# Bounds of the later batches' x taken five steps behind their loads instead of three, with two steps more per batch

## The chip, the cores and the metric

The kernel runs on one core of one Trainium2 chip. The metric is the device time of one execution in microseconds (us). Three timed runs of the kernel before gave 1472.26, 1482.52 and 1481.33 us, median 1481.33. The profile shown below is of a separate execution that took 1473.78 us, 1472.0 us of it between its first and its last instruction.

The names of the engines: PE is the matrix engine (PEld its weight loads), DVE, ACT and POOL are the vector, scalar and GpSimd engines, SP is the engine whose queue issues every DMA of this kernel (SPq).

## The reference

```python
def reference(...):                      # x: (8, 3136, 256) float32
    F = (filt_r + 1j * filt_i)[None]     # filter over 1569 frequencies
    x = np.fft.irfft(np.fft.rfft(x, axis=1) * F, n=3136, axis=1)
    X = np.fft.fft(np.fft.fft(x, axis=1), axis=2)
    u = x + np.real(X)
    un = (u - mean(u)) / sqrt(var(u) + 1e-6)          # over the 256 channels
    return u + np.maximum(un @ w_ch1, 0) @ w_ch2      # 256 -> 1024 -> 256
```

## The kernel before

There are eight batches. Each goes forward (`there`) and home (`back`), and its tokens then go through the two products of the feed-forward part in 49 groups of 256 tokens. The FFT over 3136 tokens is split into stages that are small matrix products, with the transposes between stages done by storing to DRAM and loading back.

**Forward, per batch b** (`forward1`, then `forward2`). Seven tiles of x of 512 KB are loaded (line 398, names `x_b_0` to `x_b_6`). A bound of each tile is taken: for batches 1 and 2 on ACT by a sum of squares (line 404, `xsq`), for batches 3 to 7 on DVE by a reduction to the largest magnitude (line 413 calls `absmax`, whose instruction is line 282, written to `mx`). The bounds give the power of two `sx` by which x is scaled. Then there are 14 steps: x is scaled and split in two halves of 16 bits (lines 436 and 437, `x16`), multiplied (line 442, or line 428 for batches 1 and 2, `s1`), split again (lines 444 and 445, `ast`), and stored to the DRAM tensor `d1` (line 446 or 432). All 14 stores must have landed before the first of seven loads `at` (line 467) can read `d1` back; each of them feeds two `spectrum` steps (lines 492 and 493, product `s2`; lines 502 and 506 take it out of PSUM on DVE into `yt` and `t2`). The inverse transform follows (lines 562 to 564, `i1`, stored to `d2` as `bt`), then on the way home the loads `b2` from `d2` (line 605), the products `y` (line 628), ACT's scaling `ys` (line 637), and the stores to `dy` (line 611).

**The feed-forward part.** Group g has eight columns f. Per column there are six products `h` of 512 columns (line 839), a rectifier on ACT (line 848) and a remainder on DVE (line 849, which with line 848 releases one of two PSUM buffers of `h`), and twelve products `acc` of 256 columns (line 868). The loop over q = 8g + f (392 turns, two more to drain) writes one column of first products, one column of second products, and a few steps of the batches ahead. The group's input comes over a chain: `y` is fetched from `dy` (line 698), the channel transform `mix` (line 711) is added on DVE (line 721), normalised (`st`, `mv`, `sb`, `un`, `u16`), and transposed by a DMA (line 815, `ut`).

**What sets the order.** `forward1` and `forward2` are generators. Between two `yield`s lies one step, and `advance` runs them to a count that grows with q, from line 1050 on in the main loop. A batch has `STEPS` steps, and the loop writes `STEPS`/49 of them per turn once it is past its start (`STEPS`/28 in the first 39 turns). What is written so is given to a scheduler that simulates a timeline; it decides the final order of each engine's instructions. Each engine executes its list in that order, so an instruction that waits holds up all behind it on its engine.

```python
XLAG = 3
FIRST = 21 + XLAG
STEPS = FIRST + PAUSE + 7 * 5                 # 63
for q in range(7 + XLAG):                     # forward1
    if q < 7: nc.sync.dma_start(raw[q], a["x"][b, q])
    k = q - XLAG
    if k >= 0: ... bound of tile k ...
    if q < 6 + XLAG: yield
```

Batch 0 has its own first stage without a lag, and idles `PAUSE + XLAG - 1` steps so that its count comes out as `STEPS` too. The loads of the feed-forward weights (`raw`, line 911) hang on step numbers of batch 0. The x tiles, the `at` tiles, the `z` tiles and half of the `raw` tiles share seven buffers.

Of the kernel before, what the change touches and what calls it, by code (L numbers as in the profile page):

```python
# [33 lines left out]


PAUSE = 4
XLAG = 3
FIRST = 21 + XLAG
STEPS = FIRST + PAUSE + 7 * 5
WAIT = 2  # L40
# [158 lines left out]
def _program(ctx, tc, nc, a, NB):  # L199
# [24 lines left out]
    def after(*keys):  # L224

        order = ExitStack()
        for k in keys:
            if k in marks:
                order.enter_context(tc.issue_after(marks[k]))
        return order  # L230
# [50 lines left out]
    def absmax(dst, src, axis=AX.X):  # L281
        nc.vector.tensor_reduce(dst, src, axis=axis, op=ALU.max, apply_absolute_value=True)
# [107 lines left out]
    def forward1(b, d1):  # L390
        raw = [xp.tile([128, 4, 256], F32, tag="big", name=f"x_{b}_{q}") for q in range(7)]
        xs = [t[:112] for t in raw]
        m = tp.tile([112, 8], F32, tag="mx", name=f"mx_{b}")
        for q in range(7 + XLAG):
            with after(("y", 1), ("un", 0)) if b == 1 and q > 2 else after(("b", 1)) if b == 1 else nullcontext():
                if q < 7:
                    with after("sp") if b > 1 else nullcontext():
                        nc.sync.dma_start(raw[q], a["x"][b, q])
                k = q - XLAG
                if k >= 0 and b in SQUARED:  # L400
# [4 lines left out]
                elif k >= 0:  # L405
                    with after("h"):
                        absmax(m[:, k : k + 1], xs[k], AX.XY)
            if q < 6 + XLAG:
                yield
# [45 lines left out]
    def forward2(b, d1, d2):  # L455
# [118 lines left out]
        for c in range(far):  # L574
            load(c)
            if b:
                yield
        for _ in range(PAUSE - far if b else PAUSE + XLAG - 1):
            yield
# [545 lines left out]
```

## Time and profile before

| | value |
|---|---|
| timed runs | 1472.26, 1482.52, 1481.33 us |
| profiled execution | 1473.78 us, span 1472.0 us |
| mean granted TensorE clock | 0.993 |
| busy PE, PEld, DVE | 1420.6, 937.4, 1066.2 us |
| busy ACT, POOL | 766.9, 533.2 us |
| DMA | 280.55 MB, 191 GB/s on the mean |

PE is busy for 97% of the span by the page. The span has three parts: some 137 us in which batch 0 and the weights are prepared, the long middle in which the batches' transforms are mixed into the feed-forward part, and from about 1300 us an end in which there is feed-forward work alone. A row that says "waited for: total, times, longest" names the engine and line that waited, and what ended the wait last.

### The profile page before, as it was taken

To read this page: it belongs to the slowest core of one execution; us is meant where nothing else is said; L and a number is where in the kernel's file an instruction comes from. 1 tells how busy PE (TensorE), PEld (TensorE's weight loads), DVE (VectorE), ACT (ScalarE), POOL (GpSimd) and SP (SyncE) were. 2 spreads that over 40 slices of the span, in tenths; PEclk is the share of its full clock that TensorE was granted. 3 is DMA by queue.
4 is the path that set the end of the run, shared out by engine and by line. 5 is a ranking of instruction groups with operands and counts; after the bars stand their busy time and mean duration, and the time that the engine had idled before them with its cause. 6 is when DMAs were issued, how large, how long until landed. Compare 5 with 4: busy or idle time off the path is not lost.

```text
span 1472.0 us, 30599 instructions
## 1 busy us (share of the span) xinstructions
PE 1420.6 (97%) x11521; PEld 937.4 (64%) x11521; DVE 1066.2 (72%) x2341; ACT 766.9 (52%) x1420; POOL 533.2 (36%) x674
## 2 busy tenths in 40 slices
PE   7988999999999999999999999999999999999998
PEld 3734566556766676567756667666766667666666
DVE  6786687387878876987768876887769786545552
ACT  4757455546456554555537564565446554344341
POOL 3840096028510771038400673028500574010110
PEclk9999999999999999999999999999999999999999
DMA  8966687879976988589775997679684997553320
GB/s 332 325 176 199 181 171 192 237 201 240 205 226 170 217 194 232 159 214 234 163 239 157 233 203 213 182 200 249 153 248 139 212 220 160 140 140 96 87 58 29
DMA packets 445331, 280.55 MB, mean 191 GB/s; under 512 B 218944, under 2 KB 410752, under 8 KB 445184
## 3 DMA queue, kind: packets, MB, share of 16 engines
q1 hardware_dynamic: 445184, 278.61, 72.4%
q8 instruction: 90, 1.47, 0.4%
q14 instruction: 57, 0.47, 0.1%
HBM read 124.88 MB, written 102.79 MB: 155 GB/s over the span
## 4 chain that ended last, share of the span: by engine, by line
PE 64%; DMA 11%; DVE 9%; issue 6%; ACT 4%; POOL 3%; SPq 3%; DVEq 0%; ACTq 0%; POOLq 0%
PE h L839 24%; PE acc L868 24%; DMA x<-x 4%; PE s L442 3%; PE y L628 3%; DMA at<-d 2%; PE mix L711 2%; DVE y L721 2%; DMA d<-ast 2%; PE s L492 1%; PE i L562 1%; DVE h L849 1%; PE i L564 1%; PE i L563 1%; PE s L428 1%
## 5 line engine op out<-in xcount | busy, mean ns | idle before, releaser
L868 PE MATMUL acc<-w2s,h 128*128 128x256 f16 x4704 | 594.6, 273 | 4.8 <-ACT h L848 3.6
L839 PE MATMUL h<-ut,w1s 128*128 128x512 f16 x2352 | 580.8, 379 | 9.8 <-DVE h L849 6.9
L868 PEld LDWEIGHTS <-h 128*128 128x128 f16 x4704 | 455.4, 98 | 149.1 <-issue 14.9
L848 ACT ACTIVATE h<-h 128x512 f16<-128x512 f32 x392 | 232.8, 594 | 376.1 <-PE h L839 368.8
L849 DVE SCALAR_TENSOR_TENSOR h<-h,h 128x512 f16<-128x512 f32 x392 | 267.5, 684 | 203.4 <-ACT h L848 201.8
L839 PEld LDWEIGHTS <-w1s 128*128 128x128 f16 x2352 | 221.0, 98 | 217.9 <-issue 27.4
L808 POOL TENSOR_TENSOR u<-un,u 128x512 f16<-128x512 f32 x94 | 108.4, 1169 | 676.5 <-ACT u L806 659.9
L721 DVE SCALAR_TENSOR_TENSOR y<-mix,alpha,y 128x508 f32<-128x508 f32 (+1 forms) x368 | 156.0, 475 | 4.1 <-PE mix L711 2.6
L510 POOL TENSOR_TENSOR yt<-yt,t 128x224 f32<-128x224 f32 x112 | 76.4, 682 | 136.1 <-DVE t L506 88.4
L803 ACT ACTIVATE un<-y,sb 128x256 f32<-128x256 f32 x196 | 101.9, 590 | 37.7 <-DVE sb L796 32.4
L516 POOL TENSOR_TENSOR y<-yt,y 128x448 f16<-128x448 f32 x105 | 108.1, 1032 | 20.9 <-ACT y L515 18.7
L637 ACT ACTIVATE ys<-y,alpha 128x512 f32<-128x512 f32 x112 | 75.9, 684 | 70.6 <-PE y L628 69.2
L570 DVE TENSOR_TENSOR bt<-i,bt 112x512 f16<-112x512 f32 x112 | 75.7, 683 | 50.1 <-ACT bt L569 49.8
L502 DVE SCALAR_TENSOR_TENSOR yt<-s,pF,ft 128x448 f32<-128x448 f32 x112 | 75.4, 674 | 25.1 <-PE s L493 19.0
L569 ACT CAST bt<-i 112x512 f16<-112x512 f32 x112 | 64.4, 583 | 53.2 <-PE i L564 47.9
L877 DVE SCALAR_TENSOR_TENSOR y<-acc,beta,y 128x512 f32<-128x512 f32 x98 | 71.1, 744 | 26.1 <-PE acc L868 26.0
L515 ACT CAST y<-yt 128x448 f16<-128x448 f32 x112 | 62.7, 563 | 36.0 <-POOL yt L511 33.5
L628 PE MATMUL y<-b,i 112*64 112x512 f16 (+1 forms) x480 | 70.4, 377 | 8.5 <-DMA b<-d 7.3
L555 POOL TENSOR_TENSOR eo<-ef,eo 128x448 f16<-128x448 f32 (+6 forms) x62 | 60.8, 984 | 44.5 <-ACT eo L554 43.1
L506 DVE SCALAR_TENSOR_TENSOR t<-s,pF,ft 128x448 f32<-128x448 f32 x112 | 75.4, 674 | 0.0
L534 POOL TENSOR_TENSOR ef<-yt 128x224 f32<-128x224 f32 x112 | 74.2, 681 | 1.8
L511 POOL TENSOR_TENSOR yt<-yt,t 128x224 f32<-128x224 f32 x112 | 73.7, 660 | 0.5 <-DVE mv L781 0.5
(131 smaller groups left out, 1663.2 us busy)
## 6 DMA issues: line engine op xcount, KB each, us to landing
x<-x SPq DMA_DIRECT2D x56, 512.0 KB
at<-d SPq DMA_DIRECT2D x56, 512.0 KB
b<-d SPq DMA_DIRECT2D x56, 512.0 KB
d<-ast SPq DMA_DIRECT2D x112, 224.0 KB
d<-bt SPq DMA_DIRECT2D x112, 224.0 KB
out<-y SPq DMA_DIRECT2D x98, 256.0 KB
y<-dy SPq DMA_DIRECT2D x92, 256.0 KB
dy<-ys SPq DMA_DIRECT2D x208, 112.0 KB
```

Source lines behind the costliest of these rows:

```text
L510: nc.gpsimd.tensor_tensor(yh[:, 0], yh[:, 0], t2v[:, 1], op=ALU.subtract)
L516: last = half(b, hf == 1).tensor_tensor(ylo, ytv, yhi, op=ALU.subtract)
L570: marks["low"] = nc.vector.tensor_tensor(bt[:, :, 1], p, bt[:, :, 0], op=ALU.subtract).ins
L628: marks["i2"] = nc.tensor.matmul(p[64 * h : 64 * h + 64, js], i2[:, t, h, i], bt[:, o + js.start : o + js.stop, h], start=i == 0, stop=i == 1,
L637: nc.scalar.activation(ys[:, o : o + 2], p, AF.Copy, scale=al[:, 2:3])
L721: nc.vector.scalar_tensor_tensor(out, p, al, y, op0=ALU.mult, op1=ALU.add)
L803: nc.scalar.activation(un[:m, k], y[:m, t, k], AF.Identity, bias=sb[:m, i, 1:2], scale=sb[:m, i, 3:4])
L808: marks["u16", g] = low.tensor_tensor(u16[:m, :, :, 1], unv, u16[:m, :, :, 0], op=ALU.subtract).ins
L839: marks["pe"] = nc.tensor.matmul(p[:, c0 : c0 + n].rearrange("p (t k q) -> p t k q", k=2, q=m), w1s[:, d, hw, 128 * f : 128 * f + 128], ut ...
L848: nc.scalar.activation(h[:, 0, :nt], p[:, :nt], AF.Relu)
L849: marks["h"] = nc.vector.scalar_tensor_tensor(h[:, 1, :nt], p[:, :nt], 0.0, h[:, 0, :nt], op0=ALU.max, op1=ALU.subtract).ins
L868: nc.tensor.matmul(acc[:m, k], h[:, hh, c0 : c0 + m], w2s[:, f, hw], start=f == 0 and k == 0 and i == 0, stop=f == 7 and k == 1 and i == 2,)
```

## The change

It raises the lag between the load of an x tile and its bound from three steps to five, for batches 1 to 7; `FIRST` and `STEPS` follow (63 becomes 65), and batch 0 idles for two steps more.

```diff
 PAUSE = 4
-XLAG = 3
+XLAG = 5
 FIRST = 21 + XLAG
 STEPS = FIRST + PAUSE + 7 * 5
```

No instruction is added or removed: on each engine the same instructions stand in another order. Three places follow. Line and operation come first in a row, then what is written, what is read, and the shape; the last number of a name is a buffer's.

The first is DVE at the bounds of batch 4, amid the columns of group 15. Before:

```order
L849 SCALAR_TENSOR_TENSOR h16_15_0_7853<-h_15_0_7846,h16_15_0_7853 128x512
L282 TENSOR_REDUCE mx_4_7810<-x_4_0_7803 112x1
L849 SCALAR_TENSOR_TENSOR h16_15_1_7897<-h_15_1_7890,h16_15_1_7897 128x512
L877 SCALAR_TENSOR_TENSOR y_14_6561<-acc_14_0_7608,beta_95,y_14_6561 128x512
L877 SCALAR_TENSOR_TENSOR y_14_6561<-acc_14_1_7609,beta_95,y_14_6561 128x512
L282 TENSOR_REDUCE mx_4_7810<-x_4_1_7804 112x1
L849 SCALAR_TENSOR_TENSOR h16_15_2_7937<-h_15_2_7930,h16_15_2_7937 128x512
L282 TENSOR_REDUCE mx_4_7810<-x_4_2_7805 112x1
L849 SCALAR_TENSOR_TENSOR h16_15_3_7972<-h_15_3_7965,h16_15_3_7972 128x512
L282 TENSOR_REDUCE mx_4_7810<-x_4_3_7806 112x1
L849 SCALAR_TENSOR_TENSOR h16_15_4_8014<-h_15_4_8007,h16_15_4_8014 128x512
```

And of the change:

```order
L849 SCALAR_TENSOR_TENSOR h16_15_0_7853<-h_15_0_7846,h16_15_0_7853 128x512
L849 SCALAR_TENSOR_TENSOR h16_15_1_7896<-h_15_1_7889,h16_15_1_7896 128x512
L877 SCALAR_TENSOR_TENSOR y_14_6561<-acc_14_0_7608,beta_95,y_14_6561 128x512
L877 SCALAR_TENSOR_TENSOR y_14_6561<-acc_14_1_7609,beta_95,y_14_6561 128x512
L849 SCALAR_TENSOR_TENSOR h16_15_2_7935<-h_15_2_7928,h16_15_2_7935 128x512
L282 TENSOR_REDUCE mx_4_7810<-x_4_0_7803 112x1
L282 TENSOR_REDUCE mx_4_7810<-x_4_1_7804 112x1
L849 SCALAR_TENSOR_TENSOR h16_15_3_7972<-h_15_3_7965,h16_15_3_7972 128x512
L282 TENSOR_REDUCE mx_4_7810<-x_4_2_7805 112x1
L849 SCALAR_TENSOR_TENSOR h16_15_4_8012<-h_15_4_8005,h16_15_4_8012 128x512
```

The first bound moved behind two more columns, the second behind one, the third behind one; the last of the seven (not shown) stands behind one column more. Batches 6 and 7 look alike; in batch 3 the first bound moves by two columns and the last by none; in batch 5 none moves by more than one and the first and last not at all. The loads of x stand in the same places of SP's list, but for the seventh, which goes ahead of one load of `b2`, in batches 3 to 7.

The second is ACT at the bounds of batch 2 (`xsq_2_0` to `xsq_2_6`), amid the columns of group 4, with the first scalings of batch 1 on its way home (`ys_1_0`). Before:

```order
L848 ACTIVATE h16_4_2_3537<-h_4_2_3530 128x512
L404 ACTIVATE xsq_2_0_3315,mx_2_3275<-x_2_0_3268 112x1024
L637 ACTIVATE ys_1_0_3352<-y_1_0_3353,alpha_1_2161 128x512
L637 ACTIVATE ys_1_0_3352<-y_1_1_3363,alpha_1_2161 128x512
L404 ACTIVATE xsq_2_1_3345,mx_2_3275<-x_2_1_3269 112x1024
L404 ACTIVATE xsq_2_2_3348,mx_2_3275<-x_2_2_3270 112x1024
L848 ACTIVATE h16_4_3_3601<-h_4_3_3594 128x512
```

And of the change:

```order
L848 ACTIVATE h16_4_2_3525<-h_4_2_3518 128x512
L848 ACTIVATE h16_4_3_3595<-h_4_3_3588 128x512
L848 ACTIVATE h16_4_4_3637<-h_4_4_3630 128x512
L404 ACTIVATE xsq_2_0_3344,mx_2_3275<-x_2_0_3268 112x1024
L404 ACTIVATE xsq_2_1_3414,mx_2_3275<-x_2_1_3269 112x1024
L637 ACTIVATE ys_1_0_3348<-y_1_0_3349,alpha_1_2161 128x512
L637 ACTIVATE ys_1_0_3348<-y_1_1_3359,alpha_1_2161 128x512
L404 ACTIVATE xsq_2_2_3416,mx_2_3275<-x_2_2_3270 112x1024
```

Both the bounds and the first scalings of batch 1 moved back by two columns; the seventh bound moved from behind column 6 of group 4 to behind column 0 of group 5. On PE the first product `y_1_0` moved from behind the third `h` column of group 4 into its sixth.

The third is DVE where the first spectrum of batch 5 (`yt_5_0`) is taken out, amid the last columns of group 23 (in both kernels the last remainder of the stage before, `ast_5_13`, stands just ahead of `h16_23_4`). Before:

```order
L849 SCALAR_TENSOR_TENSOR h16_23_6_11241<-h_23_6_11234,h16_23_6_11241 128x512
L780 BN_STATS st_25_11157<-y_25_10903 128x6 x2
L781 BN_AGGR mv_25_11156<-st_25_11157 128x2 x2
L792 RECIPROCAL sb_25_11166<-sb_25_11166 128x4
L793 SCALAR_TENSOR_TENSOR sb_25_11166<-sb_25_11166 128x4
L849 SCALAR_TENSOR_TENSOR h16_23_7_11300<-h_23_7_11293,h16_23_7_11300 128x512
L794 SCALAR_TENSOR_TENSOR sb_25_11166<-mv_25_11156,sb_25_11166 128x4
L795 SCALAR_TENSOR_TENSOR sb_25_11166<-sb_25_11166 128x4
L796 SCALAR_TENSOR_TENSOR sb_25_11166<-mv_25_11156,sb_25_11166 128x4
L502 SCALAR_TENSOR_TENSOR yt_5_0_11180<-s2_5_0_0_11181,pF_115,ft_91 128x448
```

And of the change:

```order
L849 SCALAR_TENSOR_TENSOR h16_23_6_11215<-h_23_6_11208,h16_23_6_11215 128x512
L780 BN_STATS st_25_11157<-y_25_10881 128x6 x2
L781 BN_AGGR mv_25_11156<-st_25_11157 128x2 x2
L792 RECIPROCAL sb_25_11166<-sb_25_11166 128x4
L793 SCALAR_TENSOR_TENSOR sb_25_11166<-sb_25_11166 128x4
L502 SCALAR_TENSOR_TENSOR yt_5_0_11180<-s2_5_0_0_11181,pF_115,ft_91 128x448
```

The spectrum now stands ahead of the remainder of column 7. On PE the products between the last `s1` of a batch and its first `s2` change with it. In batch 4 they were 18 `h`, 46 `acc` and 4 `y` (and 16 small ones of `mix`), and are 15, 35 and 4; in batch 5 they were 23, 52 and 8, and are 19, 36 and 4; in batch 6 they were 17, 36 and 8, and are 18, 46 and 4; in batch 7 they were 21, 52 and 8, and are 18, 37 and 4.

## Rows read from the trace of the kernel before

**Rows 1.** Busy time by stretch: start and end (us), length, then for PE, PEld, DVE, ACT and POOL the busy us with the count of instructions, then the granted clock, the DMA share and GB/s. The first row is the middle, the second the end without transforms, the third lies in the first stage of batch 7.

```profile
137.00:1300.00 1163.00, 1137.58 (x9454) 762.37 (x9454) 878.84 (x1926) 622.04 (x1156) 456.46 (x578) 1.00 0.79 198
1300.00:1460.00 160.00, 160.00 (x1162) 107.99 (x1161) 82.65 (x199) 58.48 (x108) 13.62 (x12) 1.00 0.30 79
1120.00:1140.00 20.00, 20.00 (x127) 12.12 (x126) 19.77 (x46) 12.77 (x22) 0.00 (x0) 1.00 0.46 133
```

**Rows 2.** Waits of PE between 137 and 1472 us, all that are listed: who waited for whom, then us in total, times, and the longest.

```profile
PE s L492 <- DMA at<-d: 7.0, 9, 1.9
PE h L839 <- DVE h L849: 4.9, 5, 1.7
PE i L562 <- DMA z<-y: 4.5, 6, 1.4
PE y L628 <- DMA b<-d: 3.1, 4, 1.5
PE h L839 <- DMA ut<-u: 2.3, 2, 1.5
PE acc L868 <- ACT h L848: 2.0, 1, 2.0
PE acc L868 <- DVE y L877: 1.3, 1, 1.3
```

**Rows 3.** Waits of DVE and ACT for tiles of x in the same stretch, in the same form.

```profile
DVE mx L282 <- DMA x<-x: 21.8, 13, 4.0
ACT xsq L404 <- DMA x<-x: 7.6, 2, 5.4
```

**Rows 4.** Waits in the stretches of the bounds, one after the other: batch 2 (250 to 280 us, one row), then batch 4 (565 to 600), batch 5 (745 to 770), two rows each, then batch 6 (905 to 935) and batch 7 (1080 to 1110), one row each; PE's wait for DVE there is the last row of Rows 2.

```profile
PE y L628 <- DMA b<-d: 1.5, 1, 1.5
...
DVE mx L282 <- DMA x<-x: 5.8, 3, 2.0
PE h L839 <- DVE h L849: 2.2, 2, 1.7
...
DVE mx L282 <- DMA x<-x: 3.4, 1, 3.4
PE h L839 <- DVE h L849: 2.1, 2, 1.6
...
PE h L839 <- DVE h L849: 0.6, 1, 0.6
...
DVE mx L282 <- DMA x<-x: 5.7, 3, 4.0
```

**Rows 5.** DVE and SP in order of time at the bounds of batch 4: start us, us, engine, line, operation, what is written and read with shapes, count, and in brackets the idle time ahead and what ended it. The first two are DVE's, the others SP's.

```profile
584.49 1.22 DVE L282 TENSOR_REDUCE mx<-x 112x1 f32<-112x1024 f32 x1 [2.00 <-DMA x<-x]
588.98 1.22 DVE L282 TENSOR_REDUCE mx<-x 112x1 f32<-112x1024 f32 x1 [2.02 <-DMA x<-x]
...
578.81 5.98 SPq L611 DMA_DIRECT2D dy<-ys  x6
585.14 1.00 SPq L398 DMA_DIRECT2D x<-x  x2
```

**Rows 6.** SP and ACT in order of time at the bounds of batch 2, in the same form; the first two are SP's, the last ACT's.

```profile
252.79 2.59 SPq L398 DMA_DIRECT2D x<-x  x5
269.57 0.65 SPq L398 DMA_DIRECT2D x<-x  x1
...
275.38 1.06 ACT L404 ACTIVATE xsq<-x 112x1024 bf16<-112x1024 f32 x1 [5.40 <-DMA x<-x]
```

**Rows 7.** PE's waits for the loads `at` in batch 4 (640 to 660 us), batch 5 (815 to 830), batch 6 (975 to 990) and batch 7 (1150 to 1165).

```profile
PE s L492 <- DMA at<-d: 1.6, 2, 1.0
...
PE s L492 <- DMA at<-d: 0.2, 1, 0.2
...
PE s L492 <- DMA at<-d: 1.9, 1, 1.9
...
PE s L492 <- DMA at<-d: 1.4, 2, 0.8
```

**Rows 8.** The chain of work that ended last, between 640 and 660 us (batch 4): start us, us, what, and how many instructions in a row.

```profile
643.13 2.85 DMA d<-ast
646.47 5.44 DMA at<-d
...
653.29 1.30 PE h L839 x6
654.59 1.31 PE acc L868 x12
...
658.61 0.55 PE y L628 x4
```

**Rows 9.** All products `h` of line 839: duration in ns (least, median, most), first and last start in us.

```profile
L839 PE MATMUL h<-ut,w1s x2352: 376/379/634, 126.7 to 1463.7; 128*128 128x512 f16 x196
```

**Rows 10.** Group 7 in order of time: ACT's casts `u16` and SP's transposes `ut`.

```profile
337.04 0.61 ACT L806 CAST u<-un 128x512 f16<-128x512 f32 x1
...
346.22 1.30 SPq L815 DMA_TRANSPOSE ut<-u  x1
```

**Rows 11.** SP in order of time, late in batch 0: two loads of weights, and the first loads `b2`.

```profile
64.89 1.73 SPq L911 DMA_DIRECT2D raw<-w  x2
...
80.74 1.01 SPq L605 DMA_DIRECT2D b<-d  x2
```

## The prediction

> **What bounds the kernel now.** I read the busy time by stretch first, then PE's waits, then what stands behind them. In the end stretch, where no transform is left, PE is busy 160.00 of 160 us; in the middle it is busy 1137.58 of 1163 us [rows 1]. So in the middle PE has little more to give than the waits that are listed for it, and after 137 us these are seven kinds, 25.1 us in all [rows 2]. The reader is to see in that list that no single wait is large: the loads `at` 7.0, the buffer of `h` that DVE releases late 4.9, `z` 4.5, `b2` 3.1, `ut` 2.3, and two single ones of 2.0 and 1.3. Then I looked at whom the change touches. DVE waits 21.8 us for tiles of x and ACT 7.6 us [rows 3]. These are long, but they are waits of engines that are not the bound; the question is how much of them PE feels.
>
> Batch 4 shows how it comes about. The bound of the fourth tile waits until 584.49; the next two tiles are issued only at 585.14, since six stores to `dy` occupy SP from 578.81 for 5.98 us, and the bound of the first of them waits until 588.98 [rows 5]. DVE's list is in order, so the remainder of the next `h` column (line 849) stands behind the waiting bound, and with it a PSUM buffer of `h`. One turn of the main loop takes (1463.7 - 126.7) / 391.8 = 3.41 us [rows 9], a step 49/63 of it, 2.65 us; the lag is 8.0 us now. With 65 steps a step is 2.57 us and a lag of five is 12.9 us.
>
> **The change part by part: what is taken away.** No work is added or removed, so the sum is one of waits. In batch 4 PE loses 2.2 us to the late buffers, in batch 5 2.1, in batch 6 0.6, in batch 7 1.3 behind line 877, and in batch 2 2.0 behind ACT [rows 2, 4]. In batches 4, 6 and 7 the bounds move back by one or two columns of the order, 2.6 us of pure `h` and `acc` each (1.30 + 1.31) [rows 8], while the loads keep their places, so DVE's single waits of up to 2.0 us there go, and of the 4.0 in batch 7 most: 2.2 + 0.6 + 1.3 = **4.1 us gained**. In batch 5 first and last bound stay where they were, so its 2.1 us stay. In batch 2 the seventh tile was issued at 269.57, 16.8 us behind the group of the five issued from 252.79, and ACT waited 5.40 us for it [rows 6]; it is queued behind a load `b2` and stores to `dy` that hang on the products `y_1`, and these move back as much as the bound does. I leave its 2.0 us in place; the bounds are 0 and 2.0. The same move of `y_1_0` by two columns or more lets the load of `b2` land in time: **1.5 us gained** [rows 4].
>
> **What is given back.** The bounds end later, the batch does not. Behind them come 14 steps, 14 stores, and the first load `at`, which needs all the stores; store and load took 2.85 and 5.44 us in batch 4 [rows 8], and PE already waits for that load in most batches: 1.6 us in batch 4, 0.2 in batch 5, 1.9 in batch 6, 1.4 in batch 7 [rows 7]. What covers the chain is PE's work between the last `s1` and the first `s2`, which the order gives. A column's six `h` take 1.30 us, twelve `acc` 1.31, four `y` 0.55 [rows 8], so 0.217, 0.109 and 0.138 each. Batch 4 loses 3 `h` and 11 `acc`: 0.65 + 1.20 = 1.9 us. Batch 5 loses 4, 16 and 4 `y`: 0.87 + 1.74 + 0.55 = 3.2. Batch 7 loses 3, 15 and 4: 0.65 + 1.64 + 0.55 = 2.8. Batch 6 gains 1 and 10 and loses 4: 0.22 + 1.09 - 0.55 = 0.8. As PE waits there already, a lost microsecond of cover passes through in full: 1.9 + 3.2 + 2.8 - 0.8 = **7.1 us lost**. The bounds are 0 (the chain comes earlier by as much as DVE no longer waits) and 7.1; I take 7.1, since nothing in the rows shortens a store or a load. On DVE the spectrum of batch 5 now stands ahead of a remainder of `h`, so if `s2` is late the column behind it is late too; that is the same wait, not a second one.
>
> Three smaller edits I cost at nothing. The group fed by batch 1 that had least room is group 7: its second cast `u16` ran at 337.04, and SP issued the last transpose at 346.22 behind other transfers [rows 10], so a cast two columns later has 9.2 us of queue to hide in; if that cover is gone it costs up to 4 us. Two loads of weights go ahead of two stores of `bt`; they occupied SP for 1.73 us at 64.89, and the stores are needed only by the loads at 80.74 [rows 11]. And DVE is busy 19.77 of 20 us in the first stage of batch 7 [rows 1], whose steps come 3% closer; over some 37 us of such steps in five batches that is at most 5 x 1.1, some 6 us, and nothing while PE is the later of the two; PE reads 20.00 there.
>
> Sum: -4.1 - 1.5 + 7.1 = **+1.5 us**. Against its own time that is 1473.8 + 1.5 = 1475.3 us. The three timed runs and the profiled one are 1472.26, 1473.78, 1481.33 and 1482.52, a mean of 1477.5; a median of three may fall near either end, so I set the sum on the mean: **1479.0 us**.
>
> **A rule weighed.** The rows say that PE's own waits cap any gain at 25.1 us [rows 2]. The Trainium skill (Perfetto Trace Analysis, "Identifying the Most-Contended Engine") says that the busy time of matmuls is a bad measure of what PE could still give, and that the share of weight loads is a better one. By that share the middle has 762.37 / 1163 = 65.6% against 67.5% (107.99 / 160) in the end stretch [rows 1], a ratio of 0.971, so 33 us of the middle would be slack, 8 more than the waits. The mixture of products differs between the two stretches, so I trust the list of waits; the sum by the rule is that of the first rival.
>
> **The rivals.** *Faster: PE is paced through its busy time.* If every microsecond that DVE and ACT wait delays PE, then the 29.4 us of waits [rows 3], less the 3.4 of batch 5 and the 7.6 of batch 2 that stay [rows 3, 4], give 18.4 instead of 4.1: -18.4 - 1.5 + 7.1 = -12.8, 1464.7 us, and without the loss of cover 1457.6, 1.3% faster. For it speaks the share of weight loads; against it, that DVE's wait of 5.8 us in batch 4 left PE only 2.2 [rows 4].
>
> *All clean.* The gains come, batch 2's and batch 5's included (9.7 us: 4.9 + 2.0 + 1.3 + 1.5), no cover is lost, batch 6 gains 0.8: 1467.0 us. For it speaks that the bounds' waits sit ahead of the same chain.
>
> *The loads are late, not the bounds.* SP keeps its order; what is 16.8 us behind in batch 2 or behind stores in batch 4 may stay ahead of nothing: no gain, cover lost in full, 1484.6 us.
>
> *Slower: the chain to `at` grows.* 14 stores and the first three loads come in fewer microseconds, behind the same transposes in SP's list, and the chain is longer by some microseconds in each of seven batches, on top of the lost cover. At 3 us each: 7.1 + 21 - 5.6 = +22.5, 1500 us. It decides (over 1%, 14.8 us) from (14.8 - 1.5) / 7 = 1.9 us per batch. Against it: the steps are only 3% closer.
>
> **How the numbers follow.** A measurement of this kernel can tell about 1% from no change; its own runs lie 0.7% apart. I give the forecast 0.46, late loads 0.20, all clean 0.15 (all within 1%), the growing chain 0.12, and the paced PE 0.07. So faster 0.07, same 0.81, slower 0.12. The range reaches from the clean case to the forecast with the 4 and 6 us that I costed at nothing (1479 + 10 = 1489): 1466 to 1490.
>
> **What would show it.** In the new profile DVE's wait for x should fall from 21.8 to about 5 us with the rest in batch 5, PE's wait for `h` behind DVE from 4.9 to about 2, and PE's wait for `at` rise from 7.0 to about 14. If `at` does not rise, the loss is wrong; if PE's waits stay near 25 us but the time moves by more than 10, the list of waits is not the bound I take it for. ACT's 5.4 us in batch 2 should still be there.

## The result, and the profile after

| | before | the change |
|---|---|---|
| median | 1479.37 us (14 runs, 1472.26 to 1483.77) | 1486.20 us (14 runs, 1481.73 to 1494.67) |
| ratio, with its 95% interval | | 1.0052, 1.0038 to 1.0066 |
| profiled execution | 1473.78 us, span 1472.0, clock 0.993 | 1482.74 us, span 1480.7, clock 0.991 |
| the change once more (run 5 below) | 1476.13 us (29 runs) | 1486.02 us (6 runs), ratio 1.0061, 1.0044 to 1.0078 |

The change is slower by half a per cent: 7.7 us by the first ratio (0.0052 x 1479.4), 9.0 by the second (0.0061 x 1476.1); the medians lie 6.8 and 9.9 us apart. The prediction was 1479.0 us, a loss of 1.5. The time is inside its range of 1466 to 1490 and within 1%, but the loss is five times the sum, and the wait that grew is another one than the prediction named. That the time falls into the range is luck.

The answer to [rows 2], PE's waits of the changed kernel from 137 us to the end (who waited for whom: us in total, times, longest):

```profile
PE i L562 <- DMA z<-y: 9.4, 7, 3.4
PE s L492 <- DMA at<-d: 6.4, 8, 1.7
PE h L839 <- DVE h L849: 3.3, 4, 1.4
PE acc L868 <- ACT h L848: 2.9, 2, 1.5
PE y L628 <- DMA b<-d: 2.3, 3, 0.8
PE i L562 <- DVE bt L570: 1.2, 1, 1.2
PE y L628 <- DVE t L506: 1.2, 1, 1.2
PE acc L868 <- DVE y L877: 1.1, 3, 0.7
PE i L562 <- DVE h L849: 0.9, 1, 0.9
PE s L492 <- DVE t L506: 0.6, 1, 0.6
PE s L492 <- DVE sb L796: 0.5, 1, 0.5
```

And the answer to [rows 3], the waits of DVE and ACT for tiles of x, in the same form:

```profile
DVE mx L282 <- DMA x<-x: 3.0, 2, 2.7
...
ACT xsq L404 <- DMA x<-x: 6.8, 3, 3.7
```

DVE's wait for x is nearly gone, 21.8 to 3.0 us, and PE's wait for `h` behind DVE fell from 4.9 to 3.3. But the list as a whole grew from 25.1 to 29.8 us. The wait for `at`, on which the prediction had put the loss, fell from 7.0 to 6.4. The wait for `z`, the transposed spectrum that the inverse transform reads, rose from 4.5 to 9.4. In a second trace of the same change `z` is 9.5 and `at` 8.0.

**Where `at` went.** SP in order of time at the end of batch 4's first stage, before the change (start us, us, queue, line, operation, what is written and read, count):

```profile
640.08 0.93 SPq L446 DMA_DIRECT2D d<-ast  x1
641.10 1.98 SPq L815 DMA_TRANSPOSE ut<-u  x1
643.13 0.70 SPq L446 DMA_DIRECT2D d<-ast  x1
...
646.04 1.01 SPq L467 DMA_DIRECT2D at<-d  x2
```

And after it:

```profile
647.73 1.28 SPq L815 DMA_TRANSPOSE ut<-u  x1
649.11 1.68 SPq L446 DMA_DIRECT2D d<-ast  x2
...
653.22 0.39 SPq L467 DMA_DIRECT2D at<-d  x1
```

PE's last `s1` and first `s2` there, before:

```profile
638.33 0.64 PE L442 MATMUL s<-x,s 112*112 112x512 f16 x2
...
650.29 0.20 PE L492 MATMUL s<-s,at 112*128 112x56 f16 x1 [0.96 <-DMA at<-d]
```

And after:

```profile
648.52 0.60 PE L442 MATMUL s<-x,s 112*112 112x512 f16 x2
...
657.57 0.20 PE L492 MATMUL s<-s,at 112*128 112x56 f16 x1
```

The cover was lost as foretold: from the last `s1` to the first `s2` it is 9.05 us now and was 11.96, 0.96 of them a wait. But the chain to `at` shrank with it. Before, a transpose `ut` of a group stood between the last two stores, and the first load was issued 7.7 us behind the last `s1` (646.04 - 638.33); now both transposes are ahead of both stores, and it is 4.7 us (653.22 - 648.52). In batches 5, 6 and 7 the first load also follows the last `s1` sooner than before, by 2.5, 2.5 and 3.4 us.

**Where `z` came from.** SP of the changed kernel in batch 7, behind the first `s2` at 1165.17 us:

```profile
1166.14 1.67 SPq L880 DMA_DIRECT2D out<-y  x1
1167.91 4.42 SPq L815 DMA_TRANSPOSE ut<-u  x2
1172.43 0.53 SPq L880 DMA_DIRECT2D out<-y  x1
1175.14 0.88 SPq L698 DMA_DIRECT2D y<-dy  x2
1176.13 1.25 SPq L527 DMA_TRANSPOSE z<-y  x1
1177.42 0.57 SPq L467 DMA_DIRECT2D at<-d  x1
1178.37 5.11 SPq L527 DMA_TRANSPOSE z<-y  x2
```

PE where it needs that `z`:

```profile
1184.87 0.46 PE L562 MATMUL i<-z,i 112*112 112x256 f16 x1 [3.42 <-DMA z<-y]
1185.13 0.42 PE L563 MATMUL i<-z,i 112*112 112x256 f16 x1
...
1188.59 0.27 PE L563 MATMUL i<-z,i 112*112 112x256 f16 x1
```

The first transpose `z` is issued 11.0 us behind the first `s2` (1176.13 - 1165.17). In the list two fetches of `y` (line 698) stand ahead of it, and SP issues nothing from 1172.96 to 1175.14, since the fetch waits until the stores to `out` have read its buffer out. The row of SP's waits that says so (us in total, times, longest), and below it the one of the kernel before:

```profile
SPq L698 <- DMA out<-y: 2.1, 1, 2.1
...
SPq L698 <- DMA out<-y: 2.2, 1, 2.2
```

So SP stood still at this place before the change too. There one of the fetches stood ahead of the transposes and one behind; SP, then PE's first `s2` and its first product of the inverse transform:

```profile
1165.22 1.05 SPq L880 DMA_DIRECT2D out<-y  x2
1168.59 0.37 SPq L698 DMA_DIRECT2D y<-dy  x1
1169.00 2.62 SPq L527 DMA_TRANSPOSE z<-y  x2
...
1172.29 0.63 SPq L698 DMA_DIRECT2D y<-dy  x1
```

```profile
1157.67 0.20 PE L492 MATMUL s<-s,at 112*128 112x56 f16 x1 [0.65 <-DMA at<-d]
...
1175.91 0.27 PE L562 MATMUL i<-z,i 112*112 112x256 f16 x1
```

The first transpose was no sooner then, 11.3 us behind the first `s2` (1169.00 - 1157.67), and PE did not wait. Two things differ. The inverse step needs the second transpose as well. It was issued at 1170.3, 12.7 us behind the first `s2`; now it follows both fetches and a load `at`, is issued 13.2 us behind (1178.37), and takes 6.46 us to land, as the chain of work that ended last has it (start us, us, what):

```profile
1178.37 6.46 DMA z<-y
```

And PE comes to the inverse step 16.3 us behind the first `s2` (1184.87 - 3.42 - 1165.17), where it was 18.2 (1175.91 - 1157.67): 29 `h` and 48 `acc` lie between, where it was 30 and 55. Cover was lost here as well; with the old 18.2 us some 1.5 of the 3.42 us would be left, as an estimate from these rows.

PE waits 3.42 us, and what follows runs at half speed: the reader compares 0.42 us with 0.27 for the same matmul.

The granted clock there, by stretch (start and end, length, PE busy with its count, granted clock, DMA share, GB/s):

```profile
1185.20:1188.20 3.00, 3.00 (x16) 0.54 1.09 283
1188.80:1191.80 3.00, 3.00 (x35) 1.00 0.82 206
```

### The profile page after: what moved, and what is told of

The parts are those of the page before. It is cut to its first block, busy times and chain, and to the rows that moved or that the text cites. A ratio compares the mean times of both kernels' runs of the same rounds, so it can differ in the third digit from the quotient of the medians.

```text
span 1480.7 us, 30627 instructions
## 1 busy us (share of the span) xinstructions
PE 1426.2 (96%) x11521; PEld 939.5 (63%) x11521; DVE 1072.8 (72%) x2341; ACT 765.2 (52%) x1420; POOL 533.1 (36%) x674
## 5 line engine op out<-in xcount | busy, mean ns | idle before, releaser
L510 POOL TENSOR_TENSOR yt<-yt,t 128x224 f32<-128x224 f32 x112 | 76.5, 683 | 145.9 <-DVE t L506 102.2
L877 DVE SCALAR_TENSOR_TENSOR y<-acc,beta,y 128x512 f32<-128x512 f32 x98 | 71.4, 743 | 21.8 <-PE acc L868 20.7
L562 PE MATMUL i<-z,i 112*112 112x256 f16 x224 | 62.8, 280 | 15.7 <-DMA z<-y 9.4
```

What stands on the lines that cost most here:

```text
L510: nc.gpsimd.tensor_tensor(yh[:, 0], yh[:, 0], t2v[:, 1], op=ALU.subtract)
```

## The experiments

The readings compete under letters. **A**: the gain of the later bounds is real, and the loss is cover between spectrum and inverse transform. **B**: the loss is a sum of a few single collisions in the lists of SP, POOL and DVE, which any shift of the order makes and removes; a collision is a place where two chains cross in one in-order list, and the one that stands behind comes late. **C**: late bounds as such. **D**: steps 3% closer. **E**: late bounds in batches 4 to 7 alone. Where an expectation gives a letter another sense, it says so. Ratios are to the kernel before on the same chip. A half-clock stretch is one with a granted clock of 0.50.

**1. The lag alone**, against the kernel before:

```diff
-                k = q - XLAG
-                if k >= 0 and b in SQUARED:
+                for k in range(q - 5, q - 4 if q < 9 else 7):
+                    if k < 0:
+                        continue
+                    if b in SQUARED:
...
```

> Bounds taken five steps behind their loads, but no step more per batch: 63 steps, the bounds of tiles 4, 5 and 6 are taken together in the last step of the first stage. Theory A (the gain of later bounds is real; the loss is that the first spectrum starts later while the inverse transform stays, so PE waits for z): DVE's wait for x falls to 3 to 8 us, PE's wait for z stays near 4.5, time 4 to 7 us below before, ratio 0.995 to 0.998. Theory B (the order is so tuned that any shift costs several us): ratio 1.003 to 1.006, with waits of other kinds. Theory C (the later bounds themselves do the harm, since stores and casts behind them get late): ratio 1.004 to 1.008, z near 9.

Measured: 1476.68 us, ratio 0.9999 (0.9985 to 1.0014). Two rows of its trace, in which PE's and DVE's lines are two higher than before (841 is 839):

```profile
PE i L564 <- DMA z<-y: 4.6, 4, 2.6
PE h L841 <- DVE h L851: 3.6, 6, 1.0
```

DVE's wait for x is 4.8 us. The waits move as A said, but the time doesn't: later bounds save 17 us of DVE's waiting and nothing that can be measured. A, B and C all miss the time.

**2. The steps alone**, against the change:

```diff
-XLAG = 5
-FIRST = 21 + XLAG
+XLAG = 3
+REST = 2
+FIRST = 21 + XLAG + REST
...
             if q < 6 + XLAG:
                 yield
+        for _ in range(REST):
+            yield
...
```

> Lag three as before, but two empty steps behind the last bound, so that a batch has 65 steps and its first scaling starts where the change puts it. Theory A: nothing gained at the bounds (DVE's wait for x near 22 us), cover lost as in the change, z near 9 us: 9 to 14 us above before, ratio 1.006 to 1.009. Theory B: 3 to 7 us above before. Theory C: within 2 us of before.

Measured: 1476.94 us, 1.0001 (0.9986 to 1.0016), DVE's wait for x 23.0 us, PE's for `z` 4.6. A misses by 9 us and B by more than 3; it is as C says, which missed run 1. Neither part of the change does anything alone; the two together cost half a per cent.

**3. The two steps at the end of a batch**, against the kernel before; the two `yield`s stand behind the last step of `forward2`:

```diff
-STEPS = FIRST + PAUSE + 7 * 5
+STEPS = FIRST + PAUSE + 7 * 5 + 2
...
+        yield
+        yield
```

> Lag three, and the two empty steps at the end of each batch's forward part instead of behind the bounds: 65 steps, so the steps are as close as in the change, but the first stage, the spectrum and the inverse transform all start earlier by up to two steps. Theory A: the distance from spectrum to inverse transform is what counts, and it isn't shortened by a later start, but the steps are 3% closer: within 4 us of before. Theory B: 3 to 7 us above. A theory D, that 65 closer steps as such cost the time (DVE and POOL are saturated in these stretches): 5 to 9 us above before, z near 9.

Measured: 1487.58 us, 1.0071 (1.0048 to 1.0094). It is 10 us above before, and the wait for `z` is 3.7 us: A, B and D all miss.

```profile
PE s L492 <- DMA at<-d: 8.5, 8, 2.1
PE h L841 <- DMA ut<-u: 8.1, 3, 3.9
```

The same number of steps in another place moves the loss to `ut`, 8.1 us against 2.3 before. The mean granted clock of its six runs was 0.9865 against 0.9917 for before; (0.9917 - 0.9865) x 1478 is 7.7 us, by this estimate most of the loss.

**4. A control**: the kernel before with a constant of the main loop that sets how far ahead the way home is written, and has no part in bounds or steps.

```diff
-SOON = 994
+SOON = 980
```

> The kernel before with one unrelated planner constant moved a little (SOON 980 instead of 994), so that some instructions stand in another order and nothing of the bounds or the steps is touched. Theory A: within 3 us of before, ratio 0.998 to 1.002. Theory B: 3 to 7 us above before, as the order of before is a tuned one.

Measured: 1481.80 us, 1.0029 (1.0017 to 1.0042). This is B's ground: an edit without any purpose costs 4.3 us, about half of what the change does.

**5. The change once more.**

> The changed kernel once more, unaltered, for a second trace and for the granted clock of before and after on one chip. All theories: ratio 1.0035 to 1.0070. If its loss is a fixed property of the order, the waits for z of 3.4 us in batch 7 and 3.1 us in batch 2 stand again at the same places; if they are accidents of one execution they move, and the loss then lies in the clock (mean 0.990 against 0.992, 2 to 3 us) and in other waits.

Measured: 1486.02 us, 1.0061. The waits stand again at their places, 3.3 us in batch 7 and 2.9 in batch 2: they belong to the order. The half-clock stretches do not all stand again: the wait in batch 3 came with one this time and not the first time, the wait in batch 2 the first time and not this time.

**6 and 7. Late bounds in some of the batches only**, 65 steps in all; `LATE` is (1, 2, 3) in the one and (4, 5, 6, 7) in the other:

```diff
+        lag = XLAG if b in LATE else XLAG - 2
         for q in range(7 + XLAG):
...
-                k = q - XLAG
+                k = q - lag if q - lag < 7 else -1
```

> 65 steps in every batch; bounds five steps behind the load in batches 1, 2 and 3 alone, and three steps behind with two empty steps after them in batches 4 to 7. Theory A (late bounds cost where ACT takes them, in batches 1 and 2, since the loss of the change had built up by batch 3): 4 to 7 us above before, ratio 1.003 to 1.005. Theory B (accidents of the order, one per displaced stretch, no place of their own): 1 to 4 us above before here and in the counterpart alike. Theory E (they cost in batches 4 to 7, in the saturated stretches): within 2 us of before.

> The counterpart: 65 steps in every batch; bounds five steps behind the load in batches 4 to 7 alone, three and two empty steps in batches 1 to 3. Theory A: 4 us below before to no change, since the waits of DVE for x go (near 3 us left in batches 4 to 7) and batches 1 to 3 keep their order. Theory B: 1 to 4 us above. Theory E: 4 to 7 us above.

Measured: 1480.44 us, 1.0027 (1.0012 to 1.0042), and 1482.45 us, 1.0044 (1.0028 to 1.0061). Both halves cost: 4.0 and 6.5 us by the ratios. B has the first at the edge of its range and misses the second, E has the second and misses the first, A misses the second. Read with runs 2 and 5 they tell where each wait of the inverse transform belongs (us that PE waits at its line; in batch 2 all for `z`, but for 3.5 us behind DVE where two numbers stand):

| stretch | steps alone | late in 1 to 3 | late in 4 to 7 | the change, twice |
|---|---|---|---|---|
| batch 2 | 4.6 | 4.3 | 0.9 and 3.5 | 3.7, 4.0 |
| batch 3 | 0 | 1.1 | 0 | 2.0, 2.5 |
| batch 7 | 0 | 0 | 3.4 | 3.4, 3.3 |

Batch 2's comes with the 65 steps, whatever the bounds; before it was 1.3. But run 2 has it in full, 4.6 us and a half-clock stretch behind it, and is no slower than before: that this wait costs the change its time is not shown. Batch 3's and batch 7's come only where the bounds of that batch are late. A, with one cause for all, has fallen, and E with it.

**8. The control of the change**: the changed kernel with the same edit.

```diff
-SOON = 994
+SOON = 980
```

> The changed kernel with the unrelated constant of the other control moved by the same 14 (SOON 980). Theory A and E: within 4 us of the change, 3 to 11 us above before. Theory B: it may fall anywhere between 0 and 12 us above before, and the control of before, which lost 4.3 us by the same edit, says that 4 us of difference between two orders need no reason in the bounds.

Measured: 1474.31 us, 0.9986 (0.9969 to 1.0002). With this constant the change is faster than its partner, by 0.0043 (1.0029 - 0.9986), where it was slower by 0.0052 to 0.0061. A and E miss, and B, which had put it from 0 to 12 us above before, misses by 2.

**9 and 10. A third value for both kernels.**

```diff
-SOON = 994
+SOON = 1030
```

> The kernel before with the unrelated constant at 1030 instead of 994, a third order for the pair of kernels. Theory B: anywhere between 5 us below and 10 us above before. Theory A: within 4 us of before, as the constant has no part in the bounds or the steps.

> The changed kernel with the same constant at 1030. Theory A: 4 to 12 us above its partner, since the change loses whatever the constant. Theory B: the difference to its partner has no fixed sign; it was +7 to +10 at 994 and -7 at 980, and lies here anywhere between -10 and +10.

Measured: 1496.42 us, 1.0133 (1.0104 to 1.0161), and 1493.52 us, 1.0108 (1.0081 to 1.0135). The intervals overlap, so here the change does nothing that can be told. The constant alone moves the kernel before by 1.3%, more than twice what the change does, and further than A or B had it. The waits, however, differ as the prediction had it: `at` is 3.9 us in the one and 14.5 in the other, while `z` falls from 11.6 to 7.6. That the order around it decides which wait takes the lost cover is how I read this; no run shows it.

**11. One collision undone**: the fetches of `y_39` behind batch 7's first two transposes `z`; two rows of SP's list go behind three others (two `z` and a load `at`), and nothing moves on any other engine.

```diff
-                with after(("un", 0)) if g == 2 else after(("out", g - 4)):
+                with after(("un", 0)) if g == 2 else after(("out", g - 4), ("z", 0)) if g == 39 else after(("out", g - 4)):
```

> The changed kernel with one edit of order: the two fetches of y_39 (line 698), which in its SP list stand ahead of the first two transposes z_7_0 and wait for stores of out, are issued behind them. No other engine's order moves. Theory B (the loss of the change is a sum of a few single collisions in SP's and POOL's lists, each with a half-clock stretch behind it): PE's wait of 3.5 us for z in batch 7 goes, and with it the half-clock stretch that stood behind it, 3.4 us long and so worth 1.7: 4 to 6 us below the change, ratio to before 1.001 to 1.004. Theory A (the cover between spectrum and inverse transform is too short by itself): the wait is only shared out anew, within 2 us of the change.

Measured: 1480.68 us, 1.0013 (0.9995 to 1.0032), 5.5 us below the change by its medians. SP in batch 7:

```profile
1173.73 0.53 SPq L880 DMA_DIRECT2D out<-y  x1
1174.35 1.30 SPq L527 DMA_TRANSPOSE z<-y  x1
1175.71 0.59 SPq L467 DMA_DIRECT2D at<-d  x1
1176.43 1.62 SPq L527 DMA_TRANSPOSE z<-y  x1
1178.49 0.90 SPq L698 DMA_DIRECT2D y<-dy  x2
```

PE's only wait from 1100 to 1200 us is now one of 0.6 us for `at`. The clock where it had been 0.54:

```profile
1184.00:1190.00 6.00, 6.00 (x60) 4.53 (x58) 5.34 (x17) 3.48 (x8) 5.91 (x8) 1.00 1.06 274
```

The first `z` follows the store to `out` at once instead of 3.2 us behind it (1176.13 - 1172.96), the wait is gone and the clock is whole. The price of this collision is shown: 5.5 us (from 3 to 10 by the intervals), 3.4 of them the wait, about 1.4 the clock ((1 - 0.54) x 3.00 us), B's figure. PE comes to the inverse step no later than in the change, 16.1 us behind its first `s2`, and has its `z` there; so the lost cover alone makes no wait in batch 7, as the fetch ahead alone made none in the kernel before. What is left, 1.0013, can't be told from nothing.

**12. A second one undone**, on top of it: group 7's casts `u16` (line 808) and transposes `ut` (line 815) behind `z_2_1`.

```diff
+            if (g, t) == (7, 0):
+                marks["y7"], marks["z7"] = marks["ylo"], marks["z", 1]
+            with after("y7") if g == 7 else nullcontext():
...
+                with after("z7") if g == 7 else nullcontext():
```

> The edit of the fetches of y_39, and a second one of the same kind: group 7's two casts u16 on POOL and its two transposes ut on SP, which in the changed kernel stand between the last casts and transposes of z_2_1, go behind them. Theory B: PE's wait of 3.1 us for z in batch 2 goes too, and the half-clock stretch behind it: 4 to 5 us below the kernel with the first edit alone, ratio to before 0.998 to 1.001; at worst 2 us of it come back as a wait of h for ut_7. Theory A: no more than 1 us below the first edit alone.

Measured: 1485.64 us, 1.0059 (1.0036 to 1.0082), back where the change was. PE's waits from 320 to 420 us:

```profile
PE i L562 <- DMA z<-y: 3.4, 3, 2.1
PE h L843 <- DMA ut<-u: 3.3, 1, 3.3
```

B missed. In batch 2 both chains are needed at the same turn of the loop; put one ahead and PE waits for the other.

**13. A third**, on top of 11: group 13's casts and transposes behind `z_3_0`.

```diff
-                marks["ylo"] = last.ins
+                marks["ylo"] = marks["ylo", ch] = last.ins
...
+            with after(("ylo", 0)) if g == 13 else nullcontext():
...
+                with after(("z", 0)) if g == 13 else nullcontext():
```

> The changed kernel with the fetches of y_39 behind z_7_0, and with group 13's two casts u16 on POOL and two transposes ut on SP behind z_3_0 again, about where the kernel before had them; in the changed kernel they stand ahead of z_3_0. Unlike group 7's, they are needed only eight columns later. Theory B (single collisions): PE's wait of 2.1 us in batch 3 goes, with the half-clock stretch that stood behind it in two of three traces: 2 to 4 us below the kernel with the first edit alone (1480.7), ratio to before 0.998 to 1.000. If it comes back as another wait, as in batch 2: within 1 us of 1480.7 or above.

Measured: 1479.67 us, 1.0011 (0.9995 to 1.0026), no gain that can be told. Between 480 and 530 us PE's inverse step now waits 1.5 us for DVE (`mv`, line 781), where the second trace of the change had 2.0 us for DVE (`yt`, line 502) and the first 2.0 us for `z`. The traces don't agree on what PE waited for in batch 3. My reading of that collision is not borne out, and its cause is left open.

**14. The diff of 11 in the kernel before**, where there was no such wait; there it moves one fetch.

> The kernel before with the fetches of y_39 behind z_7_0. There one of the two fetches stood ahead, and PE had no wait for z in batch 7. Theory B: nothing to remove, within 1.5 us of before, ratio 0.999 to 1.001. If the edit is good in itself: 2 to 5 us below.

Measured: 1476.00 us, 0.9993 (0.9977 to 1.0008). As B says.

**15. The diff of 11 in the kernel of run 8**, whose trace had the wait.

> The changed kernel with the unrelated constant at 980 (1474.3 measured) and the fetches of y_39 behind z_7_0. Its trace shows a wait for z of 2.8 us in batch 7 with a half-clock stretch behind it. Theory B: 3 to 5 us below 1474.3, that is 1469.5 to 1471.5, ratio to before 0.993 to 0.997, faster than both kernels. If the wait only moves: 1473 to 1476.

Measured: 1471.22 us, 0.9949 (0.9930 to 0.9968), below run 8 by 3.1 us in the medians, which are from two chips, or 5.5 by the ratios, and faster than both kernels of the case. From 1100 to 1200 us PE waited 2.6 us for `z` in run 8, and here only 0.3 us, for `at`. In run 8 both fetches stood ahead as well, but PE came to the inverse step 18.0 us behind the first `s2`, as in the kernel before: there the collision made the wait without lost cover.

**16. More distance everywhere**: each chunk's `fold` ahead of its inverse steps.

```diff
-                (c, spectrum, 0), (c, spectrum, 1), (c - 2, inverse1, 0), (c - 2, inverse1, 1),
+                (c, spectrum, 0), (c, spectrum, 1),
                 (c - 1 if c < 7 else c - 2 if c == 8 else -1, fold, None),
+                (c - 2, inverse1, 0), (c - 2, inverse1, 1),
...
-    folds = {FIRST + PAUSE + (4, 9, 14, 19, 24, 29, 34)[ch]: 224 * ch + 224 for ch in range(7)}
+    folds = {FIRST + PAUSE + (4, 7, 12, 17, 22, 27, 32)[ch]: 224 * ch + 224 for ch in range(7)}
```

> The changed kernel with each chunk's fold issued ahead of its inverse steps instead of behind them, so that an inverse step stands one step (2.6 us) further from its spectrum. Theory A (the cover between spectrum and inverse transform is what was lost): the waits for z fall from 9.4 to 2 to 4 us and the time to 1476 to 1481. Theory B: every list is shuffled again, so that some collisions go and others come: anywhere from 1472 to 1490.

Measured: 1483.38 us, 1.0040 (1.0025 to 1.0054). `z` fell only to 6.7, and the waits for `h` behind DVE rose to 6.5 and those for `b2` to 3.6. A's remedy doesn't help. B's range of 18 us would have held almost any time.

## Why the prediction was wrong

**The bound: right.** The listed waits of PE carry the difference, though not alone. The spans differ by 8.7 us, the lists by 4.7. For the rest there are two candidates: the changed trace has a second half-clock stretch, worth about 1.4 us, and the same product `h`, late in batch 0, starts at 133.65 us where it was 131.78.

**The gain, -4.1 and -1.5: mis-sized.** DVE's wait for x fell to 3.0 (about 5 foretold), PE's for `h` behind DVE to 3.3 (2 foretold), that for `b2` from 3.1 to 2.3, that behind line 877 from 1.3 to 1.1. That is 2.6 of the 5.6 us. Run 1, which has the later bounds and nothing else, is worth 0.0 us, with an interval of 2 us to either side. The step from "PE loses 2.2 us to the late buffers" to a gain of as much took each wait out of the list as if PE met nothing else behind it.

**The lost cover, +7.1 on `at`: the step that failed.** It read "nothing in the rows shortens a store or a load". True, but SP's list could shorten the way from one to the other, and did. The cover fell as foretold, in batch 4 by 1.95 us without the wait (11.96 - 0.96 - 9.05; 1.9 foretold). But the first load `at` follows the last `s1` 3.0 us sooner there, because a group's transpose no longer stands between the last stores, and 2.5 to 3.4 us sooner in the batches behind. The prediction held the groups' chain fixed against the stages; the change slides the two past each other. Its own test ("If `at` does not rise, the loss is wrong") came out against it: 6.4 and 8.0 us in the two traces, about 14 foretold. In its place stands PE's wait for `z`, 4.5 us before and 9.4 now, 3.42 of it in batch 7. The prediction counted the cover ahead of the spectrum and none behind it.

**What was costed at nothing.** Group 7, at "up to 4 us", was a right place to look: its casts and transposes meet batch 2's spectrum, and PE waits there for `z` (3.7 and 4.0 us in the two traces, 1.3 before) or, with the order turned, for `ut` (run 12). What the transposes of a group stand ahead of was not asked, only whether they come late themselves. What that is worth is open: run 2 has this wait in full and loses nothing. Batch 7's collision, about 5 us by run 11, was in no term, and it is most of the loss; the place of its two fetches could be read in SP's new order. The +1.5 us is thus the difference of two terms that both failed, and the term that counts is missing.

**The rivals.** The late loads (1484.6 us) come nearest to the measured time, by luck: DVE's wait for x went from 21.8 to 3.0, so the loads were not late. Slower by the chain to `at` didn't happen; the loads came 3 us sooner in batch 4. Paced PE and all clean fail with run 1. ACT's 5.4 us in batch 2 did not stay: the sum for x is 6.8 us, but the longest is 3.7.

**Shown and argued.** Shown are batch 7's collision and its price (runs 11, 14, 15), that batch 2's comes with the steps and that turning it round doesn't help (2, 6, 7, 12), and that the change has no sign of its own: +0.52 to +0.61% at one value of an unrelated constant, -0.43% at the second, -0.25% and not to be told from nothing at the third. Not shown is how batch 7's wait divides between the fetches and the lost cover: run 11 takes it away by the fetches alone, and no run gives the cover back. Only argued is that collisions of this kind make up the rest, if there is a rest; batch 3's was not traced to its end. As a general theory B does poorly: it missed runs 1, 2, 3, 7, 8, 9, 12 and 13, and in 10 and 16 its ranges were too wide to fail. What stands is the one collision that was undone.

## What to carry to other kernels

When a stage is moved by a column or two in a schedule of in-order lists, ask of each queue which other chain it slides past, and read the new order where they cross: the waits may move there, not to where the cover was counted. Count the cover behind the stage as well as ahead of it: in batch 7 PE came to its next need 2 us sooner. Before crediting or blaming a change for half a per cent, run it and the old kernel again with an unrelated constant moved; where that control moves as much as the change, the sign of the change says nothing about its idea, and it pays to look for single collisions: undoing one by moving two rows gained about 0.4% in runs 11 and 15. A small edit beside a collision is not costed at nothing until it is asked who stands behind it.

## What the hardware showed that I had not expected

A wait of PE can be paid again in clock. Behind the wait for `z` in batch 2 of the changed kernel the granted clock is 0.50, the lower level of 1.2 GHz, and then whole again (start and end, length, then PE, PEld, DVE, ACT and POOL busy, granted clock, DMA share, GB/s):

```profile
352.20:355.00 2.80, 2.80 (x11) 1.58 (x11) 1.24 (x5) 0.59 (x1) 0.00 (x0) 0.50 0.98 263
356.00:360.00 4.00, 4.00 (x27) 2.19 (x26) 3.69 (x8) 2.57 (x5) 1.82 (x3) 1.00 1.19 200
```

From 137 us on the trace of the kernel before has one such stretch, behind the wait of 2.0 us for ACT in batch 2:

```profile
278.20:281.00 2.80, 2.80 (x11) 1.24 (x10) 1.27 (x4) 0.75 (x2) 0.00 (x0) 0.50 0.96 264
```

2.80 us of work at half speed is worth 1.4, so where this happens a wait of 3 us costs nearer to 4.5; the prediction priced waits at their length. The Trainium skill (TensorE: Matmul & The Clock Gate, "HAM oscillation — how this bites in real kernels") describes a wait for a DMA after which the next products start at the lower clock; the row at 352.20 us agrees. It does not happen behind every wait: in the second trace of the change PE waits 2.9 us at the same place, and the granted clock from 352.20 to 355.00 us is 1.00. The kernel's own scatter goes with the clock in part: of the changed kernel's 14 runs the slowest had the lowest (1494.67 us, 0.986) and the fastest the highest (1481.73 us, 0.993), but another run at 0.993 took 1486.01 us.
